# The second batch's projection moved from step 33 to step 36 of the first batch's second product

## The chip, the cores and the metric

The kernel runs on one core of a Trainium2 chip. The metric is the device time of one execution in us. Each run's record marks it as fast or slower. In the profiles PE is the tensor engine, PEld its weight loads, DVE the vector engine, ACT the scalar engine, POOL GpSimd, SP the engine that issues the transposing transfers. Tiles named ps_* are the tensor engine's accumulators; p_a to p_d are copies of them; kp and vp are the projected keys and values, kT and qT the transposed keys and queries.

## The reference

Eight batches of attention in which keys and values are first projected from 1024 rows to 64, and then a feed-forward with a squared ReLU:

```python
k_proj = einsum('ks,bhsd->bhkd', E, k);  v_proj = einsum('ks,bhsd->bhkd', F, v)
attn = softmax(q @ k_proj^T / 8);        x = attn @ v_proj        # then 8192 x 512
h = maximum(x @ w_in, 0);                out = (h * h) @ w_out    # d_ff = 2048
```

## The kernel before

The program is a list of steps for the tensor engine, and tables that hang the attention of the next batch on those steps. The work of an entry comes before the matmuls of its step. For the first batch, steps 0 to 31 are the first product of its two halves, 32 to 46 the second product of the first half:

```python
# steps 32, 33, 34, 35:  ps_y (8 matmuls), ps_x (4), ps_y (6), ps_y (2), then ACT copies ps_y to p_a
# steps 36, 37 (ps_z), 38, 39 (ps_y again), ...  up to 46
second = [p1a, p2a, p1b, p1c] + lohi(p5) + lohi(p6) + lohi(p3) + lohi(p7) + [p2b]   # ... + lohi(p4)

def project(self, in_ffn_bank=0):        # 16 matmuls, K and V rows in the two halves of one bank
    ps = self.ps["kv"] = ffn_psum("ps_kv") if in_ffn_bank else att_psum([P, C], F32)
    ...
    for i in range(NI):
        nc.tensor.matmul(ps[0:KP, :], lhsT=ET[:, i, :], rhs=kv[:, :, i, :], ...)
        nc.tensor.matmul(ps[KP:P, :], lhsT=FT[:, i, :], rhs=vv[:, :, i, :], ...)

def copy_kp(self):                       # DVE: kp; then SP: transpose of kp
    ...
    nc.sync.dma_start_transpose(out=self.kT[:], in_=self.kp[:]...)
def transpose_q(self):                   # SP: transpose of Q, a DMA
    nc.sync.dma_start_transpose(out=self.qT[:], in_=self.Q[:]...)
def copy_vp(self): ...                   # ACT, twice

BATCH_1 = {
    33: "project 1", 34: "copy_kp, transpose_q, copy_vp", 37: "copy_v_down",
    48: "scores 0, scores 1, exponentials 0", 49: "exponentials 1",
    ...
WEIGHTS = {25: "T1 0", 26: "T1 1", 28: "T2 0", 30: "T2 1", 34: "T3 0", 35: "T3 1", 38: "T4 0", 39: "T4 1"}
LOADS = {0: {31: 1, 35: 2}, 1: {14: 3, 56: 4}}    # step: which batch's K, V, Q are loaded
```

K, V and Q have one buffer each, so the loads of the third batch wait for the transpose of the second batch's Q. WEIGHTS are differences of weights that the vector engine makes.

The softmax here doesn't subtract the row's maximum and nothing guards it: scores larger than these inputs give would overflow.

Of the kernel before, what the change touches and what calls it, by code (L numbers as in the profile page):

```python
# [20 lines left out]
def kernel(  # L21
# [57 lines left out]
    def regroup_psum():  # L79
        mixed_stack.close()  # L80
        ffn_home.clear()
        for pool in mixed:
            ffn_pools.remove(pool)
        att_pools.append(mixed_stack.enter_context(psum_pool("mps", 1)))
# [21 lines left out]
    def load(name, src, b):  # L106
        t = qkv_pool.tile([P, H, NI * D], BF16, name=name)
        nc.gpsimd.dma_start(t[:], rows(src, b))
        return t
# [54 lines left out]
    def E_and_F():  # L164
        for t, src, copy in ((ET, e_f32[0], nc.vector.tensor_copy), (FT, e_f32[1], nc.scalar.copy)):
            e_bf = soft_pool.tile([KP, S], BF16, tag="expT", name="e_bf")
            copy(e_bf[:], src[:])
            ps = ffn_psum("ps_E", (P, NI, KP), BF16)
            view = e_bf[:].rearrange("k (p i) -> k i p", i=NI)
            for i in range(NI):  # L170
                nc.tensor.transpose(ps[:, i, :], view[:, i, :], ident[0:KP, 0:KP])
            copy(t[:], ps[:])
# [7 lines left out]
    def combine_weights(q4, name):  # L180
        js = slice(4 * q4, 4 * q4 + 4)
        o, a, b = {"T1": (T1, W12, W11), "T2": (T2, W22, T1), "T3": (T3, W22, W12), "T4": (T4, W21, T2)}[name]
        nc.vector.tensor_tensor(out=o[:, js], in0=a[:, js], in1=b[:, js], op=ALU.subtract)
# [4 lines left out]
    class Attention:  # L188
# [273 lines left out]
        55: "normalize 1 1",  # L462
    }
    BATCH_1 = {
        33: "project 1", 34: "copy_kp, transpose_q, copy_vp", 37: "copy_v_down",
        48: "scores 0, scores 1, exponentials 0", 49: "exponentials 1",
        51: "scores 2, scores 3, exponentials 2", 52: "exponentials 3",
        55: "sums 0, sums 1, logs 0, logs 1, inverses 0", 57: "inverses 1",
# [30 lines left out]
    def calls(table, n):  # L499
        for c in filter(None, table.get(n, "").split(", ")):  # L500
            name, *args = c.split()
            yield name, [int(a) for a in args]
# [266 lines left out]
    with tc.manual_schedule(engines=ORDERED):  # L769
        batches = {0: Attention(0, Q_first, K_first, V_first)}  # L770

        def load_batch(b):

            if b < B:
                order = [("K_sb", k), ("V_sb", v), ("Q_sb", q)]
                order = order[2:] + order[:2] if b in (2, 3) else order
                t = {n: load(n, src, b) for n, src in order}
                batches[b] = Attention(b, t["Q_sb"], t["K_sb"], t["V_sb"])


        LOADS = {0: {31: 1, 35: 2}, 1: {14: 3, 56: 4}}

        E_and_F()
        batches[0].first_stages()
        for b in range(B):
            tables = {0: BATCH_1, 1: BATCH_2, B - 2: LAST_PIECES, B - 1: {}}
            for n, g in enumerate(ffn_groups(b, batches[b].xT)):
                if b == 0:
                    for name, args in calls(SECOND_HALF, n):
                        getattr(batches[0], name)(*args)  # L790
                    for name, args in calls(WEIGHTS, n):
                        combine_weights(args[0], name)
                for name, args in calls(tables.get(b, PIECES), n):
                    of = batches.get(b + (2 if name[0] == "+" else 1))
                    if of:
                        getattr(of, name.lstrip("+"))(*args)
                if n in LOADS.get(b, {30: 0}):
                    load_batch(LOADS.get(b, {30: b + 3})[n])
                g()
            if b == 0:  # L800
                batches[1].normalize(1, 1)
            if b == 1:
                regroup_psum()
# [30 lines left out]
```

## Time and profile before

| | before |
|---|---|
| median of the first 3 runs | 481.50 us (481.39 to 481.93) |
| span of the profiled execution | 480.1 us, tensor engine busy 98% |
| product starts (first ps_y matmul) | 51.72 us |
| V of the second batch lands | 53.27 us |
| first ps_z matmul | 56.45 us |
| first scores of the second batch | 67.46 us |

### The profile page before, as it was taken

Reading aid. Unit: us, or ns where it says so; the run is one execution under the profiler, and the core shown is the slowest. Engines: PE = TensorE matmul, PEld = TensorE weight load, DVE = VectorE, ACT = ScalarE, POOL = GpSimd, SP = SyncE. Lnnn points to the kernel's source line nnn. Section 1 sums busy time; section 2 is a strip of 40 time slices with the busy share of each in tenths; the row PEclk is TensorE's granted clock in tenths of the full one; section 3 lists DMA queues with packets and bytes.
Section 4 is the critical chain, followed back from the end, with each engine's and each line's share of the span. In section 5 each row is a group of like instructions: output and inputs, shape, how many; then the busy total and the mean of one; then the engine's idle time right before and its main releaser. Section 6 shows DMA issues by size and latency. Waiting matters only on the chain.

```text
span 480.1 us, 8400 instructions
## 1 busy us (share of the span) xinstructions
PE 468.3 (98%) x3630; PEld 294.0 (61%) x3630; DVE 314.4 (65%) x382; ACT 247.8 (52%) x365; POOL 34.8 (7%) x48
## 2 busy tenths in 40 slices
PE   4899999999999999999999999999999999999997
PEld 2544686475664756648475574846657475766656
DVE  1478955554957659584695838857485856959383
ACT  2387544758416564375634756156652666334352
POOL 6440020020020100001000100000000000000000
PEclk9999999999999999999999999999999999999999
DMA  9999989579979997209952199223402002020202
GB/s 159 203 204 207 168 183 200 138 117 226 168 113 239 141 209 140 88 1 147 223 81 89 19 178 206 49 87 62 127 1 82 6 1 88 1 89 0 89 1 87
DMA packets 72789, 55.46 MB, mean 116 GB/s; under 512 B 33968, under 2 KB 64944, under 8 KB 72752
## 3 DMA queue, kind: packets, MB, share of 16 engines
q0 software_dynamic: 30624, 29.36, 39.8%
q1 hardware_dynamic: 42128, 25.56, 21.2%
q8 instruction: 28, 0.46, 0.4%
q14 instruction: 9, 0.07, 0.0%
HBM read 59.24 MB, written 16.78 MB: 158 GB/s over the span
## 4 chain that ended last, share of the span: by engine, by line
PE 88%; DMA 9%; POOL 1%; issue 0%; ACT 0%; POOLq 0%
PE ps_h L507 23%; PE ps_y L527 22%; PE ps_att L507 17%; PE ps_z L527 16%; DMA V_sb<-in_v_dram 7%; PE ps_kv L216 2%; PE ps_att L258 2%; PE ps_att L527 2%; DMA w_in<-in_moe_w_in_dram 2%; PE ps_att L243 2%; PE ps_x L527 1%; PE ps_kv L217 0%; POOL V_sb L120 0%; POOL K_sb L120 0%; POOL Q_sb L124 0%
## 5 line engine op out<-in xcount | busy, mean ns | idle before, releaser
L571 DVE TENSOR_TENSOR hsq<-h_relu 128x1024 bf16<-128x1024 f32 x123 | 149.9, 1222 | 79.1 <-ACT h_relu L563 62.5
L507 PEld LDWEIGHTS <-w_in 128*128 128x128 bf16 x1024 | 99.6, 98 | 117.9 <-issue 1.9
L507 PE MATMUL ps_h<-xT,w_in 128*128 128x512 bf16 x640 | 147.8, 379 | 0.2 <-DVE xT L390 0.2
L527 PEld LDWEIGHTS <-s 128*128 128x128 bf16 x1024 | 99.1, 98 | 16.2 <-issue 4.8
L561 ACT ACTIVATE h_relu<-ps_h 128x512 f32<-128x512 f32 x159 | 92.3, 596 | 24.2 <-PE ps_h L507 24.0
L507 PE MATMUL ps_att<-xT,w_in 128*128 128x512 bf16 x384 | 90.7, 379 | 0.0
L527 PEld LDWEIGHTS <-hsq 128*128 128x128 bf16 x768 | 73.8, 98 | 16.5 <-issue 6.0
L563 ACT ACTIVATE h_relu<-ps_att 128x1024 f32<-128x1024 f32 x48 | 49.1, 1023 | 55.4 <-PE ps_att L507 55.4
L527 PE MATMUL ps_y<-T,s 128*128 128x256 bf16 x480 | 57.7, 273 | 0.0
L521 DVE TENSOR_TENSOR s<-hsq 128x1024 bf16<-128x1024 bf16 x64 | 43.5, 683 | 0.0
L285 DVE TENSOR_TENSOR xT<-ps_att,rs 128x1024 bf16<-128x1024 f32 x28 | 33.0, 1214 | 0.6 <-PE ps_att L258 0.6
L657 DVE TENSOR_TENSOR o_sb<-ps_z,p_b 128x512 f32<-128x512 f32 x16 | 11.1, 691 | 33.4 <-PE ps_z L527 27.5
L527 PE MATMUL ps_z<-T,s 128*128 128x256 bf16 x256 | 30.9, 273 | 0.0
L527 PE MATMUL ps_z<-w_out,s 128*128 128x256 bf16 x256 | 30.7, 273 | 0.0
L527 PE MATMUL ps_y<-w_out,hsq 128*128 128x256 bf16 x240 | 30.5, 273 | 0.0
L651 ACT COPY o_sb<-ps_y 128x512 f32<-128x512 f32 x15 | 8.7, 578 | 40.2 <-PE ps_y L527 40.1
L527 PE MATMUL ps_y<-T,hsq 128*128 128x256 bf16 x240 | 29.0, 273 | 0.0
L250 ACT ACTIVATE expT<-ps_att 128x1024 bf16<-128x1024 f32 x28 | 27.7, 1029 | 1.9 <-PE ps_att L243 1.9
L657 DVE TENSOR_TENSOR o_sb<-ps_y,p_d 128x512 f32<-128x512 f32 x15 | 10.4, 690 | 21.4 <-issue 19.7
L651 ACT COPY p_b<-ps_y 128x512 f32<-128x512 f32 x15 | 8.8, 588 | 27.0 <-PE ps_y L527 27.0
L521 DVE TENSOR_TENSOR s<-s,hsq 128x1024 bf16<-128x1024 bf16 x32 | 21.8, 685 | 0.4
L521 DVE TENSOR_TENSOR s<-hsq,s 128x1024 bf16<-128x1024 bf16 x32 | 21.8, 683 | 0.0
(86 smaller groups left out, 277.4 us busy)
## 6 DMA issues: line engine op xcount, KB each, us to landing
out_dram<-o_sb SPq DMA_DIRECT2D x30, 512.0 KB, 3.4
K_sb<-in_k_dram POOLq DMA_DIRECT2D x7, 1024.0 KB, 10.7
V_sb<-in_v_dram POOLq DMA_DIRECT2D x7, 1024.0 KB, 17.8
Q_sb<-in_q_dram POOLq DMA_DIRECT2D x7, 1024.0 KB, 10.4
w_out<-in_moe_w_out_dram POOLq DMA_DIRECT2D x4, 512.0 KB, 13.8
w_in<-in_moe_w_in_dram POOLq DMA_DIRECT2D x7, 256.0 KB, 10.4
K_sb<-in_k_dram POOLq DMA_DIRECT2D x2, 512.0 KB, 8.3
out_dram<-o_sb SPq DMA_DIRECT2D x3, 256.0 KB, 2.1
```

Of the source, the lines that this page charges most:

```text
L216: nc.tensor.matmul(ps[0:KP, :], lhsT=ET[:, i, :], rhs=kv[:, :, i, :], start=f, stop=l)
L243: nc.tensor.matmul(ps[o, bank, :], lhsT=self.kT[r, 2 * pr + j, :], start=True, stop=True, rhs=self.qT[r, NT * (2 * pr + j):NT * (2 * pr + ...
L250: nc.scalar.activation(e[:], self.ps["s", pr][:], AF.Exp, scale=SCALE)
L285: nc.vector.tensor_tensor(out=self.xT[:, 2 * g + e].rearrange("p a n t -> p a (n t)"), in0=self.ps["v", g, e][:], in1=self.rs[g][:], op=AL ...
L507: nc.tensor.matmul(ps[:], lhsT=w_in_blk(cb, fb), rhs=xT[:, cb, :, 2 * ch:2 * ch + 2], start=(cb == 0), stop=(cb == NCB - 1),)
L521: nc.vector.tensor_tensor(out=s[o][:, js], in0=x, in1=y, op=op)
L527: nc.tensor.matmul(ps[tb] if len(ps) == 2 else ps[0][:, tb], lhsT=lhs[:, j, tb * P:(tb + 1) * P], rhs=rhs[:, j], start=first and n == 0 an ...
L561: nc.scalar.activation(r[:, n], ps[:], AF.Relu)
L563: nc.scalar.activation(r[:], st["h"][:], AF.Relu)
L571: multiply = lambda: nc.vector.tensor_tensor(out=o, in0=r[:], in1=r[:], op=ALU.mult)
L651: nc.scalar.copy(to[:, t], ps)
L657: nc.vector.tensor_tensor(out=to[:, t], in0=ps, in1=more[:, t], op=ALU.add)
```

## The change

The intent is to give the loads three steps more before the tensor engine asks for V, and to keep what depends on the projection, and the third batch's loads, in the same distance behind it.

```diff
     BATCH_1 = {
-        33: "project 1", 34: "copy_kp, transpose_q, copy_vp", 37: "copy_v_down",
+        36: "project 1", 37: "copy_kp, transpose_q, copy_vp", 39: "copy_v_down",
...
-        LOADS = {0: {31: 1, 35: 2}, 1: {14: 3, 56: 4}}
+        LOADS = {0: {31: 1, 38: 2}, 1: {14: 3, 56: 4}}
```

In the compiled programs the orders on SP and GpSimd (which issues the loads) are the same before and after. What changes is the place of the 16 matmuls; on the vector engine kp comes behind the second half of T3.

## The prediction

> **What bounds the kernel now.** I read the page's busy times first, then the waits of each engine, then the chain that ended last, and last the timeline from 50 to 70 us and from 91 to 95 us, where the moved pieces run.
>
> ```profile
> PE 468.3 (98%) x3630; PEld 294.0 (61%) x3630; DVE 314.4 (65%) x382; ACT 247.8 (52%) x365; POOL 34.8 (7%) x48
> PEclk9999999999999999999999999999999999999999
> ```
>
> The busy times and the granted clock: the tensor engine is busy 468.3 of 480.1 us at full clock, and the vector engine, next, only 314.4. So the kernel is a queue of matmuls, and a change that removes no matmul can gain only what the tensor engine loses by waiting. The sum of its idle times in the view of waits is about 8 us, nearly all before 25 us (5.2 us of it is the wait for the copy of E). Only one of them lies where the change acts:
>
> ```profile
> PE ps_kv L217 <- DMA V_sb<-in_v_dram: 0.2, 1, 0.2
> 30.38 22.89 DMA V_sb<-in_v_dram
> 53.27 0.04 issue
> 53.31 0.38 PE ps_kv L217
> ```
>
> The first line is from the waits (us in total, times, longest); the other three are neighbours in the chain that ended last (start, duration, what). The load of the second batch's V, issued at 30.38 us, lands at 53.27 us, and the projection's first V matmul starts 0.04 us later. From there to the end the chain is matmul after matmul. So the projection of the second batch stands in the queue slightly before its data is there. The timeline shows what that costs:
>
> ```profile
> 52.68 0.40 PE L216 MATMUL ps_kv<-K_sb,ET 128*64 128x512 bf16 x1
> 53.31 0.38 PE L217 MATMUL ps_kv<-V_sb,FT 128*64 128x512 bf16 x1 [0.23 <-DMA V_sb<-in_v_dram]
> ...
> 55.13 0.61 PE L527 MATMUL ps_x<-w_out,hsq 128*128 128x256 bf16 x4
> ```
>
> The idle column says only 0.23 us, because it counts from the modelled end of the K matmul (0.40 us long). Matmuls here overlap: K and V matmuls of a pair start together and pairs follow each 0.215 us. The true loss is found by comparing with the same 16 matmuls of the next batch, which wait for nothing:
>
> ```profile
> 92.59 0.40 PE L216 MATMUL ps_kv<-K_sb,ET 128*64 128x512 bf16 x1
> 92.60 0.40 PE L217 MATMUL ps_kv<-V_sb,FT 128*64 128x512 bf16 x1
> ...
> 94.44 3.63 PE L507 MATMUL ps_h<-xT,w_in 128*128 128x512 bf16 x16
> ```
>
> From the first projection matmul to the first matmul after it: 94.44 - 92.59 = 1.85 us without a wait, 55.13 - 52.68 = 2.45 us with it. **The wait costs 0.60 us**, 0.12% of the run.
>
> **What the Trainium skill says.** "TensorE: Matmul & The Clock Gate", in "The mechanism" of its Part 3, says that matmuls start and end in program order, without reordering; so a V matmul that waits holds up everything behind it. The trace agrees: ps_x, whose data had long been there, starts only at 55.13 us. "DMA: Bandwidth & Descriptors", in "Issuing engines are not separate DMA queues", says that transfers of all issuing engines share the same 16 DMA engines and interleave; here the DMA view gives 22.9 us for V because K, V and Q of the batch queue up behind the weights at about 207 GB/s, and Q lands 26.7 us after its issue at 31.66 us, at 58.36 us. The same page, in "Why a DMA increments its semaphore by 16 and not by 1", says that a transfer counts as landed only when all 16 engines have reported; that matters below: in the trace's records of the first Q transpose, 15 of 16 increments have come by 65.06 us and the last at 66.62 us.
>
> **The change part by part.** Nothing is removed and nothing added; 16 matmuls, five copies and two transposing transfers stand elsewhere in the queues. The loads of the third batch move from step 35 to 38 only because their Q buffer must follow the transpose of the old Q in program order.
>
> (1) The projection moves behind the 4 matmuls on ps_x and 8 on ps_y that now follow it (steps 33 to 35). Those take 56.45 - 55.13 = 1.32 us in the timeline, and none waits for anything: they read squares of the first half, made long before. So the projection starts at about 52.68 + 1.3 = 54.0 us, 0.7 us after V has landed. It takes 1.85 us instead of 2.45, and the product on ps_z starts at 56.45 - 0.60 = 55.85 us. **Gain on the tensor engine: 0.60 us.**
>
> (2) The copies. On the vector engine kp now comes after both halves of T3 instead of one.
>
> ```profile
> 55.23 0.68 DVE L183 TENSOR_TENSOR T<-w_out,w_out 128x1024 bf16<-128x1024 bf16 x1
> 55.83 0.68 DVE L223 CAST kp<-ps_kv 64x512 bf16<-64x512 f32 x1
> 56.54 0.29 DVE L224 COPY kp<-kp 64x512 bf16<-64x512 bf16 x1
> 56.75 0.68 DVE L183 TENSOR_TENSOR T<-w_out,w_out 128x1024 bf16<-128x1024 bf16 x1
> 56.85 1.30 SPq L226 DMA_TRANSPOSE kT<-kp  x1
> 58.41 4.83 SPq L208 DMA_TRANSPOSE qT<-Q_sb  x1
> ```
>
> The last projection matmul will end at 55.20 + 1.31 - 0.60 = 55.9 us, but the second T3 piece fills 55.83 to 56.5, so kp starts at about 56.4 us, 0.6 later, and the transpose of kp is issued at about 57.45 us. It holds the queue 1.30 us; the Q transpose follows, some 0.1 to 0.2 us after, at 58.85 to 58.95 us. Before, it waited for Q's landing (58.36 us), so it slips by only **0.45 to 0.55 us**. On the scalar engine the vp copies end near 57.8 us, just when the copy of p_d is wanted (58.40 - 0.60 = 57.80 us); ps_z is written again only at 59.95 - 0.60 = 59.35 us, so 0.6 us is spare after that 0.58 us copy. No cost.
>
> (3) The first scores of the second batch are the next place that needs what moved:
>
> ```profile
> qT<-Q_sb SPq DMA_TRANSPOSE x1, 8.2
> 67.18 0.87 POOL L108 DMA_DIRECT2D Q_sb<-in_q_dram  x1 [34.65 <-DMA qT<-Q_sb]
> 67.46 0.63 PE L243 MATMUL ps_att<-qT,kT 64*64 64x512 bf16 x8
> ```
>
> The transpose issued at 58.41 us lands 8.2 us later, at 66.6 us; the scores start at 67.46 us, so there was 0.86 us of slack. In the changed kernel the tensor engine is there at 67.46 - 0.60 = 66.86 us. If the transpose again takes 8.2 us it lands at 58.9 + 8.2 = 67.1 us, plus some 0.05 us of signalling: a **new stall of about 0.3 us**. If it takes 6.7 us, the shortest of the seven in the view of tile qT, it lands at 65.6 us and there is no stall. I count the late sixteenth report as an accident that comes back in about one case in three: 0.1 us expected.
>
> (4) The third batch's loads wait for that landing, not for their step: the queue had waited 34.65 us for it. They start at 67.18 us now, and at 66.1 to 67.7 us after. V, issued at 68.91 us, took 22.7 us and landed at 91.6 us; it is needed at 92.59 us. After the change it is needed at 92.0 to 92.3 us and lands at 90.5 to 92.1 us. Slack of about 1 us becomes 0 to 1.5 us: at most 0.1 us expected.
>
> Sum: -0.60 + 0.1 + 0.05 = **about -0.45 us**; 481.5 - 0.45 = 481.05, say **481.0 us**.
>
> **The rivals.** First, the wait moves: a stall at the scores (3), or at the third batch's projection (4), takes the place of the old one. For it: slacks of 0.86 and 1.0 us against an arrival 0.6 us earlier and a Q transpose 0.5 us later. Against it: a Q transpose of 6.7 us lands 1.3 us before it is wanted. It would make 481.2 to 481.5 us. Second, the gain is larger in ordinary runs: V's landing at 53.27 us is that of one execution, and an execution with a later V loses more before and nothing after, up to the 0.7 us of cushion. That would be 480.5 us. Third, the vector engine becomes the bound, as kp, T4 and vp bunch up. Against it: between 59.7 and 62 us it idles 2.31 us waiting for ps_z, and the T4 pieces are wanted only at the end of this chunk, after 64.75 us; no change of time. Fourth, the later loads run into other transfers and come late for the scores and projections of later batches. Against it: the later transposes and loads are placed relative to tensor-engine steps, and the next loads of V (106.20 us plus 25.1) precede their use at 133.43 us by 2 us; it would cost some tenths at most.
>
> **Range and chances.** The runs before spread from 481.39 to 481.93 us, 0.54 us, as much as the effect. The best case is 481.5 - 0.6, the worst a full new stall plus scatter, so 480.5 to 481.8 us should hold 8 in 10. Two per cent are 9.6 us, more than all idle time of the tensor engine together, so faster by that much cannot come of a move; slower by it would need a stall of 16 times the one removed. Faster 0.005, same 0.985, slower 0.01.
>
> **What would show it.** In the changed trace: no wait of L217 for V; the projection starts near 54.0 us and lasts 1.85 us to the first ps_z matmul at about 55.85; kp's cast near 56.4; the Q transpose issued near 58.9 us; the scores at 66.9 us without a wait, or up to 67.2 with one named for qT; the projection of the third batch near 92.0 us. The prediction is wrong if V lands much later than 53.3 us in most runs, if the Q transpose lands after 67.5 us, or if the matmuls of steps 33 to 35 meet a wait for a buffer that the projection's time had hidden.

## The result, and the profile after

| first comparison, 6 runs each | median | lowest to highest |
|---|---|---|
| before | 481.48 us | 481.23 to 481.93 |
| changed | 482.14 us | 481.74 to 483.76 |

The ratio is 1.0018 (95% interval 1.0003 to 1.0032). Ratios here are the mean time of one kernel's fast runs over that of the other's of the same rounds, so not quite the ratio of the medians. The change looked slower, and outside the predicted range.

Yet the profiled execution of the changed kernel, 481.74 us, shows a span of 479.9 us, 0.2 less than before. These are the busy times of its page and the top of its tensor-engine waits (us in total, times, longest):

```profile
PE 468.5 (98%) x3630; PEld 294.4 (61%) x3630; DVE 314.8 (66%) x382; ACT 247.8 (52%) x365; POOL 34.5 (7%) x48
```
```profile
PE ps_E L171 <- DVE e_bf L167: 5.6, 1, 5.6
PE ps_E L171 <- ACT e_bf L167: 0.7, 1, 0.7
```

The wait for V is gone from the list and nothing new stands after 25 us. The timeline of the changed kernel (start, duration, engine, what) shows the stretch where the pieces moved:

```profile
52.09 1.04 PE L527 MATMUL ps_y<-w_out,hsq 128*128 128x256 bf16 x8
52.96 0.60 PE L527 MATMUL ps_x<-w_out,hsq 128*128 128x256 bf16 x4
53.40 1.04 PE L527 MATMUL ps_y<-w_out,hsq 128*128 128x256 bf16 x8
54.37 0.40 PE L217 MATMUL ps_kv<-V_sb,FT 128*64 128x512 bf16 x1
54.47 0.59 ACT L651 COPY p_a<-ps_y 128x512 f32<-128x512 f32 x1 [1.25 <-PE ps_y L527]
56.22 1.92 PE L527 MATMUL ps_z<-T,s 128*128 128x256 bf16 x16
56.80 0.68 DVE L223 CAST kp<-ps_kv 64x512 bf16<-64x512 f32 x1
57.97 1.91 PE L527 MATMUL ps_y<-T,s 128*128 128x256 bf16 x16
59.26 4.84 SPq L208 DMA_TRANSPOSE qT<-Q_sb  x1
67.26 0.63 PE L243 MATMUL ps_att<-qT,kT 64*64 64x512 bf16 x8
```

The projection runs 1.85 us to the first ps_z matmul, as predicted. From the product's first matmul to ps_z it takes 56.22 - 52.09 = 4.13 us; before, from 51.72 to 56.45 us, 4.74 us before rounding. So 0.6 us is gained there, but the product began 0.37 us later than in the trace of before, where the two programs are still the same. The question is therefore not only what the change does but where a start that differs comes from, and whether the first comparison measured the change at all.

### The profile page after: what moved, and what is told of

Same layout as the page of the kernel before. It is cut to its first block, busy times and chain, and to the rows that moved or that the text cites. A ratio compares the mean times of both kernels' runs of the same rounds, so it can differ in the third digit from the quotient of the medians.

```text
span 479.9 us, 8400 instructions
## 1 busy us (share of the span) xinstructions
PE 468.5 (98%) x3630; PEld 294.4 (61%) x3630; DVE 314.8 (66%) x382; ACT 247.8 (52%) x365; POOL 34.5 (7%) x48
## 4 chain that ended last, share of the span: by engine, by line
PE 96%; ACT 1%; DVE 1%; DMA 1%; issue 0%; SPq 0%
PE ps_h L507 28%; PE ps_y L527 22%; PE ps_att L507 17%; PE ps_z L527 16%; PE ps_kv L216 3%; PE ps_att L258 2%; PE ps_att L527 2%; PE ps_att L243 2%; PE ps_x L527 1%; DMA e_f<-in_F_dram 1%; PE ps_k L301 1%; ACT expT L353 0%; DVE xT L390 0%; PE ps_fill L400 0%; DVE hsq L571 0%; ACT h_relu L561 0%
## 5 line engine op out<-in xcount | busy, mean ns | idle before, releaser
L657 DVE TENSOR_TENSOR o_sb<-ps_y,p_d 128x512 f32<-128x512 f32 x15 | 10.4, 690 | 21.4 <-issue 19.7
L651 ACT COPY p_a<-ps_y 128x512 f32<-128x512 f32 x15 | 8.8, 586 | 25.9 <-PE ps_y L527 25.7
```

Of the source, the lines that this page charges most:

```text
L651: nc.scalar.copy(to[:, t], ps)
L657: nc.vector.tensor_tensor(out=to[:, t], in0=ps, in1=more[:, t], op=ALU.add)
```

## The experiments

Three theories for a slower changed kernel. **A**: the Q transpose, now later, makes the first scores of the second batch wait. **B**: the third batch's V comes late and its projection near 92 us waits. **C**: nothing new waits; what scatters is the start-up of the kernel, which is the same in both. Later a rival **D** was added: the changed kernel itself starts later.

One number sorts the traces: the time from the product's first ps_y matmul to the start of the kernel's last matmul. It contains all that the change touches and nothing of the start-up. (The last group of 16 matmuls starts 1.64 us before that last matmul: before, 474.79 us in the timeline, so 476.43 - 51.72 = 424.71 us.)

### The changed kernel again, and three variants

**after_again**: no edit.

> The changed kernel once more, for its scatter and a second trace. Measured before: 482.14 us against 481.48. Theory A (the Q transpose of the second batch is issued 0.5 to 0.8 us later, behind kp, and lands after the tensor engine has reached the first scores): again 0.3 to 0.9 us slower than before, and in a slower execution the trace shows the first scores of the second batch waiting for qT. Theory B (the third batch's V lands late, because its loads start when the Q transpose has landed): as slow, but the wait is at the projection near 92 us, not at the scores. Theory C (no new wait; the start-up scatter of the tensor engine, which the wait for V had hidden, now comes through): wider scatter, no wait in the trace after 50 us, the projection's start scattering.

**before_kp_later**: on the kernel before, one side effect of the change alone.

```diff
-  ... 34: "T3 0", 35: "T3 1", 38: "T4 0", ...
+  ... 34: "T3 0, T3 1", 38: "T4 0", ...
```

> The kernel before, with one thing of the change alone: the second half of T3 ahead of the kp copy on the vector engine, so that kp, the transpose of kp and then the Q transpose come some 0.6 us later; the projection stays where it was. Theory A: the Q transpose starts near 59.0 us and lands at 65.6 to 67.3 us against scores at 67.46 us: 0 to 0.5 us slower than before, some executions more. Theory B: third batch's loads 0.5 us later, slack of about 1 us at the projection: 0 to 0.3 us slower. Theory C: no change, within 0.15 us of before.

**kp_first**: on the changed kernel, that side effect taken back.

```diff
-  ... 34: "T3 0", 35: "T3 1", 38: "T4 0", ...
+  ... 34: "T3 0", 38: "T3 1, T4 0", ...
```

> The changed kernel with the second half of T3 behind the kp copy, so that kp waits only for the projection; the Q transpose starts some 0.5 us earlier than in the changed kernel, near 58.4 to 58.8 us. Theory A: most of the loss is gone and part of the gain appears: 0.2 to 0.6 us faster than the changed kernel, near 481.2 us. Theory B: the same direction, since the loads follow the Q transpose: 0.3 to 0.5 us faster. Theory C: as the changed kernel, within 0.2 us.

**scores_later**: on the changed kernel, the waiter of theory A moved away.

```diff
-  48: "scores 0, scores 1, exponentials 0", 49: "exponentials 1",
-  51: "scores 2, scores 3, exponentials 2", 52: "exponentials 3",
+  49: "scores 0, scores 1, exponentials 0", 50: "exponentials 1",
+  52: "scores 2, scores 3, exponentials 2", 53: "exponentials 3",
```

> The changed kernel with both pairs of the second batch's scores, and their exponentials, one step later on the tensor engine (0.9 us and 1.75 us of other matmuls go ahead of them); the transposes stay late. Theory A: the wait for qT is covered, near 481.0 to 481.3 us, 0.6 us or more faster than the changed kernel. Theory B: no change against the changed kernel, because the third batch's loads start no earlier. Theory C: no change.

| same chip | median (lowest to highest) | ratio to before | product's first to last matmul |
|---|---|---|---|
| before (11 runs) | 482.64 (481.50 to 483.77) | | |
| after_again | 482.05 (480.92 to 483.65) | 0.9985 (0.9967 to 1.0003) | 424.12 us |
| before_kp_later | 482.04 (481.83 to 483.51) | 0.9988 (0.9972 to 1.0004) | 424.96 us |
| kp_first | 481.79 (481.13 to 481.98) | 0.9976 (0.9962 to 0.9990) | 424.12 us |
| scores_later | 481.33 (481.22 to 482.63) | 0.9974 (0.9959 to 0.9988) | 424.12 us |

Here the kernel before scatters over 2.3 us, and the sign is the other way round. By the medians alone scores_later would have confirmed theory A: it is 0.7 us below after_again. The traces say otherwise. All three kernels with the moved projection take 424.12 us, to a hundredth, scores late or not, and none waits for qT or at the third batch's projection. **A and B fall.** The median of scores_later lies low only as far as its runs started early.

Of the 1.22 us by which the product starts later in after_again than in before, 1.05 us are there by the first ps_h matmul, at 21.76 and 20.71 us. This is the second K projection of the first batch, the same 8 matmuls in both programs, first in the traced execution of before, then in that of after_again:

```profile
8.77 1.80 PE L301 MATMUL ps_k<-K_sb,ET 128*64 128x256 bf16 x8 [0.30 <-DMA K_sb<-in_k_dram]
11.54 1.06 PE L301 MATMUL ps_k<-K_sb,ET 128*64 128x256 bf16 x8
```
```profile
9.33 1.86 PE L301 MATMUL ps_k<-K_sb,ET 128*64 128x256 bf16 x8 [0.78 <-DMA K_sb<-in_k_dram]
12.28 1.91 PE L301 MATMUL ps_k<-K_sb,ET 128*64 128x256 bf16 x8
```

The first lines: K landed 0.56 us later in the second execution. The second lines: 1.06 us against 1.91 us for the same work, because the tensor engine did not yet have its full clock. The trace's clock records grant it at 10.4 us in the first execution and at 14.6 us in the second. (The page's PEclk row does not show this: it prints 9 for the time before the first record.) The Trainium skill, "TensorE: Matmul & The Clock Gate", section "What's actually happening", says that the clock opens after a window of 3.4 us of activity, and that this window runs freely and does not start with the kernel. The traces agree: full clock came anywhere between 10.4 and 16.9 us in the executions without a warm-up, and it then lasted 464.21, 467.63 or 471.04 us, in steps of 3.4 us. The product started 1.2 us later in the second execution, 52.94 us against 51.72.

before_kp_later showed something that no theory had named. Its own timeline, with the idle time and its releaser in brackets:

```profile
58.71 0.58 ACT L651 COPY p_a<-ps_y 128x512 f32<-128x512 f32 x1
59.35 1.91 PE L527 MATMUL ps_y<-T,s 128*128 128x256 bf16 x16 [0.67 <-ACT p_a L651]
```

ACT takes its work in order: p_a stood behind the vp copies, those behind kp, and the tensor engine waits to write ps_y again. This chain exists, shorter, in the kernel before too, and the change cuts it by putting p_a first. That is the reason for the next control.

**D finds no support either.** The traces of before and of the changed kernel have the same instructions in the same order on every engine up to the product's first ps_y matmul. And from the 41st ps_h matmul, near 31 us, to that ps_y matmul both kernels take 20.84 us in every trace, so a start that differs has come about before 31 us.

### Before against itself, a warm start, and an earlier projection

**before_control**: no edit.

> The kernel before against itself, to see the scatter alone, and a second trace of it. In the traces so far the time from the first matmul on ps_y to the end is 424.12 us with the projection moved and 424.71 us in the one trace with it unmoved, whatever happened earlier, while the start of that matmul moves between 51.6 and 52.9 us, together with the moment at which the tensor engine gets its full clock (10.4 to 14.6 us). Theory C (start-up scatter): the ratio lies within 0.2% of 1 by chance alone, single runs lie between 481 and 484 us, and the trace shows the V wait as long as max(0, V's landing minus the first ps_y matmul minus 0.93 us): between 0 and 0.6 us. Rival D (the change itself costs 0.5 us or more somewhere before the first ps_y matmul): before is again tighter than the changed kernel, 481.2 to 482 us.

**warm_before** and **warm_after**: nine matmuls on a constant tile ahead of everything, on the kernel before and on the changed one.

```diff
+    warm = const_pool.tile([P, 512], BF16, name="warm")
+    nc.vector.memset(warm[:], 1.0)
...
+        ps_warm = ffn_psum("ps_fill")
+        for _ in range(9):
+            nc.tensor.matmul(ps_warm[:], lhsT=warm[:, 0:P], rhs=warm[:], start=True, stop=True)
         E_and_F()
```

> The kernel before with nine matmuls on a constant tile from about 1 us on, so that the tensor engine has its full clock before the first K projection. Theory C: the start-up is shorter and steadier, the first ps_y matmul starts at 51.0 to 51.7 us in every run, so the wait for V is there each time (0.5 to 1.2 us); the time is about 481.3 to 481.7 us with a spread well under that of before. Rival D: no change of the spread.

> The changed kernel with the same nine matmuls. Theory C: with the start-up steady the move gains what the wait cost: 0.4 to 0.9 us faster than warm_before, about 480.7 us, and faster than both kernels; the trace shows no wait for V and possibly a short one for qT. Rival A (a late Q transpose eats the gain): as warm_before or slower, with a wait for qT at the first scores. Rival D: slower than warm_before by 0.5 us or more.

**project_early**: on the kernel before, the projection one step earlier.

```diff
-  33: "project 1", 34: "copy_kp, ...
+  32: "project 1", 34: "copy_kp, ...
```

> The kernel before with the projection one step earlier, ahead of the first 8 matmuls on ps_y (0.87 us): the wait for V is made longer by up to that much. If the step of the prediction that prices the wait is right, the time from the first matmul of this product to the end grows by 0.87 us where the wait was there anyway (425.6 us), and by less where V had already landed; whole runs 0 to 0.9 us slower than before, hard to see in the scatter that theory C expects. If the wait is hidden anyway, no change in the trace.

| same chip | median (lowest to highest) | ratio to before |
|---|---|---|
| before (9 runs) | 481.66 (481.36 to 482.82) | |
| before_control | 481.87 (481.49 to 483.04) | 1.0011 (0.9997 to 1.0025) |
| warm_before | 481.38 (481.07 to 481.91) | 0.9996 (0.9984 to 1.0009) |
| warm_after | 482.17 (480.73 to 482.28) | 1.0000 (0.9987 to 1.0013) |
| project_early | 482.56 (482.43 to 483.19) | 1.0022 (1.0010 to 1.0035) |

The kernel before came out 0.11% slower than itself. Its trace has **no wait for V**: V landed at 52.58 us and was wanted at 52.58. Still it takes 424.35 us, 0.23 more than the changed kernel. This is where (timeline of before_control):

```profile
51.61 1.04 PE L527 MATMUL ps_y<-w_out,hsq 128*128 128x256 bf16 x8
55.76 1.91 PE L527 MATMUL ps_z<-T,s 128*128 128x256 bf16 x16
57.09 0.59 ACT L651 COPY p_a<-ps_y 128x512 f32<-128x512 f32 x1
57.73 0.49 PE L527 MATMUL ps_y<-T,s 128*128 128x256 bf16 x3
```

Product to ps_z takes 4.15 us, as in the changed kernel. But the 16 matmuls on ps_z take 1.75 us elsewhere, so ps_y was due at 57.51 us; it starts at 57.73, just after p_a ends at 57.68. These 0.22 us appear in no idle column, since the modelled end of the last ps_z matmul covers them. In the execution that I had read, the wait for V had covered this one.

The warm-up failed as a tool. In warm_before the clock opened at 4.7 us, closed again at 8.1 and opened at 11.5. Its wait for V was 0.2 us, where 0.5 to 1.2 had been expected. In warm_after it opened only at 13.7 us, and warm_after was not faster than warm_before, where 0.4 to 0.9 us had been expected: a miss. Their traces take 424.35 and 424.11 us for the part that the change touches.

project_early was no clean measure of the wait either. In its trace F came late, the product, which now begins with the projection, started at 53.35 us, and V, landing at 53.67, was waited for only 0.36 us; the 0.87 us expected did not appear there. That all five runs lie above 482.4 us fits a floor set by V's landing, but one trace does not show that.

### V made late on purpose, and a better warm start

**late_v_before** and **late_v_after**: an unused load of three heads ahead of the second batch's V.

```diff
+        def load_extra():
+            extra = const_pool.tile([P, 3, NI * D], BF16, name="extra")
+            nc.gpsimd.dma_start(extra[:], rows(k, 1)[:, 0:3])
...
+                if b == 1:
+                    order = order[:1] + [("extra", k)] + order[1:]
...   # and load_extra() is called for "extra"
```

> The kernel before with an unused load of three heads (0.4 MB) between K and V of the second batch, so that V and Q land some 1.9 us later, whatever the start-up does. If the wait for V is priced rightly, the V wait grows to 1.6 to 3 us, and the time from the first ps_y matmul of the product to the end goes from 424.4 to about 426.1 to 427 us; whole runs 1.3 to 2.5 us slower than before, near 483.5 to 484.5 us.

> The changed kernel with the same unused load. If the change gains the smaller of the wait and the 1.31 us of matmuls moved ahead, then here it gains the whole 1.31 us: about 1.3 us (1.0 to 1.6) faster than late_v_before, with a V wait of 0.3 to 1.7 us left, and that shows in the medians through the start-up scatter. If the gain is eaten by the later Q transpose, it is under 0.6 us, and the trace names qT at the first scores of the second batch.

**warm2_before** and **warm2_after**: the nine matmuls, and four more on the constant tile after the transposes of E and after those of F.

> The kernel before with matmuls on a constant tile from 1.5 us on and more of them between the transposes of E and F and ahead of the first K projection, so that the clock is not taken back before 8 us as it was in warm_before. Start-up scatter as the cause of the spread: first ps_y matmul at 51.0 to 51.8 us, median 481.0 to 481.6 us, spread of the runs under 1 us; V wait 0.2 to 0.9 us in the trace. Else: spread as before.

> The changed kernel with the same warm-up: 0.2 to 0.7 us faster than warm2_before, near 480.6 to 481.0 us, and faster than both kernels, if the change only removes waits; 424.12 us from the first ps_y matmul to the end, no V wait. If the change costs something elsewhere, equal to or slower than warm2_before.

| same chip | median (lowest to highest) | ratio to before | product's first to last matmul |
|---|---|---|---|
| before (11 runs) | 482.49 (481.39 to 483.80) | | |
| late_v_before | 483.45 (483.39 to 485.05) | 1.0028 (1.0010 to 1.0047) | 426.30 us |
| late_v_after | 482.34 (481.72 to 482.85) | 0.9998 (0.9979 to 1.0017) | 424.47 us |
| warm2_before | 481.87 (480.88 to 483.48) | 0.9991 (0.9970 to 1.0012) | 424.35 us |
| warm2_after | 481.34 (480.87 to 482.35) | 0.9982 (0.9964 to 1.0000) | 424.11 us |

These 11 runs of before are also among the 12 of the next table.

With V late the move gains 1.11 us in the medians; 1.0 to 1.6 had been expected, and no run of one kernel overlaps the other's. Against before, late_v_before is 0.96 us slower in the medians, less than the 1.3 to 2.5 expected. The timelines, late_v_before first:

```profile
51.62 1.04 PE L527 MATMUL ps_y<-w_out,hsq 128*128 128x256 bf16 x8
54.81 0.38 PE L217 MATMUL ps_kv<-V_sb,FT 128*64 128x512 bf16 x1 [1.81 <-DMA V_sb<-in_v_dram]
57.95 0.82 PE L527 MATMUL ps_z<-T,s 128*128 128x256 bf16 x6
```
```profile
52.62 1.04 PE L527 MATMUL ps_y<-w_out,hsq 128*128 128x256 bf16 x8
55.29 0.38 PE L217 MATMUL ps_kv<-V_sb,FT 128*64 128x512 bf16 x1
57.10 0.50 PE L527 MATMUL ps_z<-T,s 128*128 128x256 bf16 x3
```

In the first the V matmul waits until 54.81 us, and product to ps_z takes 6.33 us. In the second the product started a full 1.00 us later, and ps_z still starts 0.85 us earlier, after 4.48 us: only 0.35 us of the wait is left. The whole stretch is 1.83 us shorter, but not all of that is the move. V is wanted 0.97 us after the product's start in the kernel before and 2.27 us after it in the changed one, 1.30 us later. It landed 3.15 us after that start in late_v_before and 2.62 in late_v_after, 0.53 us sooner. The waits that follow, 2.18 and 0.35 us, match the measured ones, 2.20 and 0.35 us over the 4.13 of no wait. So the mechanism of the prediction is right: **the move gains what the wait is worth, up to the 1.3 us of matmuls moved ahead of it.** No wait for qT appears.

The second warm-up held the clock, from 6.7 and 6.8 us on, but the runs scatter as before, over 2.6 us, where under 1 us had been expected. In warm2_before the tensor engine then waited 0.6 us for weights. In warm2_after_2, told of below, the clock was held from 7.05 us, but the first K came late, at 9.7 us, and the product started at 52.71 us, not before 52.0 as expected. The clock is one source of the start-up's scatter; the landing of the first loads is another.

### The first comparison repeated

**after_3**, **after_4** and **after_5** are the changed kernel, **before_control_2** and **before_control_3** the kernel before, **warm2_after_2** the second warm-up again; after_5 and before_control_3 ran on another chip.

> The changed kernel, third time. Scatter alone: ratio between 0.997 and 1.001, single runs 480.9 to 484 us, and in the trace 424.1 us from the first ps_y matmul of the product to the last matmul, with that first matmul anywhere between 51.2 and 54 us. Later start-up through the change: ratio above 1.001 and the first ps_y matmul later than 52.3 us in this trace and the next, while the control's is earlier.

> The same kernel under another name: the same expectations; how far its median lies from that of after_3 is a measure of the scatter, which I expect to be 0.2 to 0.8 us.

> The kernel before against itself: ratio 0.998 to 1.002. Scatter alone: single runs also reach 483 us; in the trace 424.3 us or more from the first ps_y matmul to the end (0.2 us for the late copy of p_a, or the V wait if that is longer).

> The changed kernel with the steady warm-up, second time: if it beats both, the ratio to before is 0.997 to 0.999, median 481.0 to 481.6 us, and the first ps_y matmul starts before 52.0 us. Else its ratio is 0.999 or more.

> The changed kernel, fourth repeat. Scatter alone: ratio 0.997 to 1.001; 424.1 us from the first ps_y matmul of the product to the last matmul in the trace, whatever the chip. A dependence on the chip: ratio above 1.001 on another chip than that of the first repeats, with that same 424.1 us and a later start of the product.

> The kernel before against itself: ratio 0.998 to 1.002; 424.3 us or more in the trace. On a chip other than that of the earlier repeats the median may again be 481.5 us with little scatter, as in the first comparison.

| | median (lowest to highest) | ratio to before |
|---|---|---|
| before (12 runs) | 482.55 (481.39 to 483.80) | |
| after_3 | 481.36 (481.23 to 482.85) | 0.9979 (0.9961 to 0.9996) |
| after_4 | 481.60 (481.15 to 482.31) | 0.9984 (0.9967 to 1.0001) |
| before_control_2 | 482.53 (481.49 to 482.83) | 1.0000 (0.9983 to 1.0018) |
| warm2_after_2 | 481.33 (480.81 to 482.33) | 0.9979 (0.9960 to 0.9998) |
| other chip: before (11 runs) | 482.37 (481.17 to 484.19) | |
| after_5 | 481.73 (481.46 to 483.68) | 0.9998 (0.9979 to 1.0018) |
| before_control_3 | 481.61 (481.39 to 482.75) | 0.9995 (0.9976 to 1.0013) |

The nine traces of the two kernels, side by side:

| trace | full clock from | product starts | V lands | product's first to last matmul |
|---|---|---|---|---|
| before | 10.4 us | 51.72 us | 53.27 us | 424.71 us |
| before_control | 12.3 | 51.61 | 52.58 | 424.35 |
| before_control_2 | 15.3 | 52.49 | 52.90 | 424.35 |
| before_control_3 | 12.6 | 51.67 | 52.67 | 424.35 |
| changed, first | 13.5 | 52.09 | 52.62 | 424.14 |
| after_again | 14.6 | 52.94 | 54.02 | 424.12 |
| after_3 | 16.9 | 53.12 | 52.52 | 424.21 |
| after_4 | 11.2 | 51.62 | 52.75 | 424.13 |
| after_5 | 11.0 | 51.86 | 52.90 | 424.13 |

The change takes 0.14 to 0.6 us off what it touches, in every pair of traces. The start of the product, which it doesn't touch, lies between 51.6 and 53.1 us, early and late with both kernels. It goes with the clock: in the five traces with full clock by 12.6 us the product starts at 51.61 to 51.86 us, in the four with full clock from 13.5 us on at 52.09 to 53.12. In before_control_2 and before_control_3 the first K landed within 0.05 us of each other, the clock opened 2.7 us apart, and the product started 0.82 us apart. All runs together: 66 of before have a median of 482.10 us (481.17 to 484.19), 30 of the changed kernel 481.72 us (480.92 to 483.76); either has a standard deviation of 0.77 us or just under it. The means differ by 0.25 us; labels shuffled at random differ by as much in about 15% of the draws. So the whole runs do not show a gain; the traces do.

warm2_after lies 0.2% under before in both of its runs (the first at the edge of the interval, and both against largely the same runs of before), but with 481.34 and 481.33 us it is level with after_3's 481.36: no version tried is shown to beat both kernels. **Why the six runs of before in the first comparison lay together, none over 481.93 us, remains open.** Of the other 60 runs 26 are that low, so six drawn from them would all be in about one of 200 draws. Chance alone is thus unlikely, but this was looked at afterwards. The record does not name the chip of that comparison. That the change costs nothing there is shown by its own trace of that chip, 424.14 us, for that execution alone, the fastest of the six; the other five have no trace.

## Why the prediction was right or wrong

- **The time and the range: wrong.** 482.14 us lay outside 480.5 to 481.8. The step that failed is the one that took the scatter from the runs before: "The runs before spread from 481.39 to 481.93 us, 0.54 us, as much as the effect." Three runs were too few: 66 runs spread over 3.0 us. In the nine traces the start-up, which the prediction did not price, moves the product's start by 1.5 us. The repeats of the same kernel gave medians of 482.05, 481.36, 481.60 and 481.73 us, three of them inside the range. That is no proof of the gain: of the three controls of the kernel before one, 481.61 us, lies inside as well. The chances for "within 2%" were right.
- **What bounds the kernel: right.** From the first scores to the last matmul every trace with the scores unmoved takes 408.96 to 408.98 us, so all that counts happens before. "At full clock", read from the PEclk row, is wrong for the first 10.4 us.
- **(1), the projection: right in its working, its size that of one execution.** "The wait costs 0.60 us" is true of that trace; in three others of the same kernel there is none, or nearly none. What the change removes there is 0.2 us of another wait, for the copy of p_a, which the prediction had not seen because the V wait covered it. So where about 0.45 us was forecast, 0.14 to 0.23 us is what the stretch loses against those three.
- **(2), the copies: right in size on the transposes.** The Q transpose was issued at 59.26 us; 58.85 to 58.95 predicted plus the 0.37 us later start. "On the scalar engine ... No cost" missed the gain from p_a going first.
- **(3), the scores: the short transpose was the exception.** The "accident" of one case in three was the rule: this Q transpose took 7.9 to 8.4 us in all 13 traces without a warm-up or an extra load (the last section has the pattern). In the changed kernel it took 8.0 us, and reached the scores at a tie: they start at 67.26 us, some 0.02 us late. after_3 lost 0.09 us there. The stall of 0.3 us did not come.
- **(4), the third batch's loads: right.** No trace waits for its V.
- **The rivals.** The first, a moved wait, was real but 0.1 us at most. The second, a larger gain in ordinary runs, was the wrong way round: the execution read had an early product and a late V, so an unusually long wait. The third and fourth did not come: the first changed trace has no tensor-engine wait after 25 us, and from the first scores on nothing changed.

## What to carry to other kernels

A wait read from one execution is a sample: before pricing its removal, ask whether both sides of the race, here the tensor engine's arrival and a load's landing, move from run to run, and take more than one trace. Below half a per cent compare a stretch of the trace that starts where the programs begin to differ, and run the unchanged kernel against itself, before believing a sign. Removing a wait also uncovers the shorter wait that it hid.

## What the Trainium skill lacked or had wrong

- "TensorE: Matmul & The Clock Gate", section "What's actually happening", calls the cost of the clock's ramp under 1% of a typical kernel, and variable from run to run. That agrees, but the page does not say how far this moves a whole kernel, nor that it hides changes of that size: with full clock from 10.4 to 16.9 us, the product started between 51.6 and 53.1 us, and the same kernel compared with itself gave 1.0011.
- The same section says that an idle window of some 3.4 us closes the clock again. In warm_before the clock opened at 4.7 us, closed at 8.1 and opened at 11.5, windows of 3.4 us, but the window that closed it was not idle: the tensor engine is busy for 2.05 us of it, 1.35 us of that with transposes, and idle for at most 1.37 us on end. So some work in a window does not keep the clock; how much, or of which kind, would is not shown.
- "Runtime: NRT & Kernel Launch", section "Instruction fetch mechanics", calls the fetch of a 16 KiB block of instructions mostly hidden. In all 20 traces one such packet of the instruction queue, 0.9 us long, starts within the second batch's Q transpose, and the later it starts, the later the transpose lands: started 0.8 us after the issue, 6.7 us (warm2_after); at 1.8 to 2.7 us, 7.2 to 7.4; at 4.2, 7.6; at 5.4 to 5.5, 7.9 to 8.0 (the changed kernel); at 6.1 to 6.3, 8.2 to 8.4 (before; 15 of 16 reports come within 6.8 us there, the last some 1.5 us after them). The next Q transpose of each trace, near 97 us, has no such packet and takes 6.6 to 6.7 us. No run moved the packet on purpose, so this is a pattern and not a tested cause; no page has it.
